# Attention and two MLPs on one Trainium2 core: the first block's first-half products in whole float32, weights and inputs split into rounded parts behind it

## The chip, the cores and the metric

The kernel runs on one core of one Trainium2 chip. The metric is the device time of one execution in microseconds (us): the median over runs of the same program. The core has a matrix engine (TensorE, in the profile PE, with its weight loads listed apart as PEld), VectorE (DVE), ScalarE (ACT), GpSimd (POOL) and SyncE (SP), which here only issues DMAs. Each engine takes its instructions strictly in the order in which the program has them; they meet by semaphores.

## What is computed

Four batches of eight heads: 512 local queries that see a window of 32 keys to both sides and 32 global keys, and 32 global queries that see everything. The result, 2176 tokens of 512 columns, goes through a first MLP with a squared ReLU and a second one with a product of two projections:

```python
x = attn_out.transpose(0, 2, 1, 3).reshape(B * S, H * D)   # 2176 x 512
h = np.maximum(x @ w_in, 0.0)          # w_in 512 x 2048
x = h * h @ w_out                      # w_out 2048 x 512
a, b = x @ w1, x @ w2                  # 512 x 1024 each
y = (a * b @ w3) @ w_out2              # 1024 x 1024, 1024 x 512
```

## The kernel before

**Arithmetic.** Nearly every product is made with operands that are split in two: a part rounded to the type float32r and the rest, subtracted in float32 and rounded too. `PASSES` lists three products of such parts (high by high, high by low, low by high); they are summed in PSUM. So one float32 product of a 128x128 weight tile with a block of columns is three matmuls. `split_w` (lines 447 to 453) splits a weight unit of 128x512: a cast on ACT (L448) and a subtraction on DVE (L449). `split_x` (552 to 556) splits an operand: a cast on ACT (L554), a subtraction on DVE (L137), and a store of both parts to `xs_d` on SP's queue (L556). The first four head pairs' scores and all products with probabilities and values are made in float32 itself.

**Weights.** They come as 64-bit words. A unit of 128x512 weights takes a load of 512 KB (`load_w`, tile `wraw`, two buffers), two ACT instructions (`conv_a`, L424 and L427), two DVE instructions (`conv_b`, L432 and L437; the second one frees the `wraw` buffer, and the load of the unit after next is issued) and an addition on POOL (`conv_c`, L506), whose result is a float32 weight in the tile `wt`; then `split_w` into a tile of the ring `u1` (16 buffers). Units 0 to 7 are the first half of `w_in`, 8 to 15 the first half of `w_out`.

**Stages.** The 2176 columns are cut into eight blocks of 256 and 288, two for each batch. Pass one takes the first half of the hidden units through all blocks: `h_unit(i, f, f)` makes unit f of block i (12 matmuls into a PSUM tile `h`, of which there are two), its ReLU (ACT L569), the square's rounded part (ACT L570), the whole square (DVE L572) and the square's low part (DVE L137). `x_unit_a(i, d)` adds up eight units into one of four output tiles (24 matmuls, PSUM tile `x`, two of them), `end_a` copies it into `st` (ACT L683) and, after the fourth, stores it to `part_d`; `split_a` splits a quarter of the next block's input. Pass two does the second half, and the second MLP follows. The columns of a batch exist once its attention is done, so `merge` interleaves the attention of the next batch, which `cycle(j)` lists pair of heads by pair, with the MLP of this one. For pairs 4 to 15 the keys and queries come in a tile `kqraw`, six loads for each pair, are split on DVE (`emit_k`: L202, L137 with 1120 columns), and POOL collects the global queries (`qgp`, L256) before PE makes the global scores `sg` and the local ones `sc`.

**What sets the order.** The code lists steps; a scheduler of the framework then puts the instructions of each engine into a fixed row by its own model, apart from a few that are held in program order. So an edit moves instructions far from where it stands. Block 0 is done while the attention of pairs 0 to 3 still runs and the weights still arrive; the tiles `wraw` and `wt` stand in a pool `cv`, which is closed behind it, and `kqraw` takes its place.

Of the kernel before, what the change touches and what calls it, by code (L numbers as in the profile page):

```python
# [9 lines left out]
F32 = mybir.dt.float32  # L10
F32R = mybir.dt.float32r
BF16 = mybir.dt.bfloat16
I32 = mybir.dt.int32
U32 = mybir.dt.uint32
AF = mybir.ActivationFunctionType
ALU = mybir.AluOpType
# [39 lines left out]
NB = 288  # L56
# [4 lines left out]
def block(i):  # L61
    i %= NBLK
    return S * (i // 2) + HALF * (i % 2), HALF if i % 2 == 0 else S - HALF
# [7 lines left out]
RUNS = (0, 16, PAIRED + 16)  # L71
# [26 lines left out]
AT_BUFS, H_BUFS, X_BUFS, P_BUFS, KQ_BUFS, ST_BUFS, HL_BUFS = 4, 2, 2, 5, 4, 6, 14  # L98
# [3 lines left out]
def attention_mlp(ctx: ExitStack, tc: tile.TileContext, kq0, kq, vw, wts, mask, ident, out_d):  # L102
    nc = tc.nc
# [3 lines left out]
    def pool(name, side="left", **kw):  # L107
        return tc.tile_pool(name=name, bufs=1, side=side, reuse_waits="tile", **kw)

    one = ctx.enter_context(pool("one"))  # L110
    sb = ctx.enter_context(pool("sb"))
# [3 lines left out]
    ps = ctx.enter_context(tc.tile_pool(name="ps", bufs=1, space=PSUM))  # L115
# [20 lines left out]
    def split_lo(eng, lo, raw, hi):  # L136
        eng.tensor_tensor(out=lo, in0=raw, in1=hi.bitcast(F32), op=ALU.subtract)  # L137
# [8 lines left out]
    def chain(o, terms):  # L146
        for k, (w, x) in enumerate(terms):
            mm(o, w, x, start=(k == 0), stop=(k == len(terms) - 1))  # L148
# [255 lines left out]
    raw_t, mid_t, w_t = {}, {}, {}  # L404
# [39 lines left out]
    def unit(tag, dtype=F32R):  # L444
        return pools[tag].tile([128, 2, 512], dtype, tag=tag, name=tag, bufs=16)

    def split_w(t, cols, raw, held=False):
        nc.scalar.copy(t[:, 0, cols], raw)  # L448
        s = nc.vector.tensor_tensor(  # L449
            out=t[:, 1, cols], in0=raw, in1=t[:, 0, cols].bitcast(F32), op=ALU.subtract  # L450
        )
        if held:
            tc.keep_in_program_order(s)
# [3 lines left out]
    def add_up(x, tag, eng):  # L457

        a11, a12, a21, a22 = (x[:, m, 256 * k : 256 * (k + 1)] for m in range(2) for k in range(2))
        s = unit(tag, F32)  # L460
        s1, s2, s3, s4 = (s[:, m, 256 * k : 256 * (k + 1)] for m in range(2) for k in range(2))
        add = eng.tensor_tensor
        add(out=s1, in0=a21, in1=a22, op=ALU.add)
        add(out=s2, in0=s1, in1=a11, op=ALU.subtract)
        add(out=s3, in0=a11, in1=a21, op=ALU.subtract)
        add(out=s4, in0=a12, in1=s2, op=ALU.subtract)
        return s

    def split_blocks(key, n, x, s, tag, held=False):

        t = []

        def third(raw):
            t.append(unit(tag))
            split_w(t[-1], slice(0, 512), raw, held)

        def last():
            if n % 2 == 0:
                half_t[tag] = unit(tag)
            (p, q, r), h, at = t, half_t[tag], 256 * (n % 2)  # L480
            split_w(h, slice(at, at + 256), x[:, 1, 256:], held)
            blocks_w[key] = {1: (p, 0), 2: (p, 256), 5: (q, 0), 6: (q, 256), 7: (r, 0), 3: (r, 256), 4: (h, at)}

        return [*(lambda raw=raw: third(raw) for raw in (x[:, 0], s[:, 0], s[:, 1])), last]

    def conv_c(n):
        _, b, m = mid_t.pop(n)
        if n >= PAIRED:
            k, u = divmod(n - PAIRED, 2)
            if u == 0:  # L490
                both_t[k] = unit("u1", F32)
                if "s" in both_t:
                    o, x, s = both_t.pop("s")
                    nc.sync.dma_start(out=both_d[o], in_=x)
                    nc.sync.dma_start(out=sums_d[o], in_=s)
            nc.gpsimd.tensor_tensor(out=both_t[k][:, u].bitcast(I32), in0=b, in1=m, op=ALU.add)
            if u == 1:
                x = both_t.pop(k)
                s = add_up(x, "u1", nc.vector)
                if k < 4:  # L500
                    both_t["s"] = k, x, s
                else:
                    for f in split_blocks(FIRST[k - 4], k, x, s, "u1"):
                        f()
            return
        nc.gpsimd.tensor_tensor(out=b, in0=b, in1=m, op=ALU.add)  # L506
        t = w_t[n] = unit(UNITS[n])
        split_w(t, slice(0, 512), b.bitcast(F32))

    def conv(n):  # L510

# [11 lines left out]
    xh, g_t = {}, {}  # L523
# [19 lines left out]
    def x_parts(i, k, n):  # L543

        t = xb_t[i, k] = fixed[4 * (i % 2) + k] if fixed else parts(NB)
        return t[:, :, :n]
# [5 lines left out]
    def split_x(i, k, src):  # L552
        t = xh[i, k] = x_parts(i, k, src.shape[-1])
        nc.scalar.copy(t[:, 0], src)  # L554
        split_lo(nc.vector, t[:, 1], src, t[:, 0])
        nc.sync.dma_start(out=of_split(i, k), in_=t.bitcast(F32))  # L556
# [5 lines left out]
    def h_unit(i, f, w):  # L562
        n = block(i)[1]
        h = ps.tile([128, 512], F32, tag="h", name="h", bufs=H_BUFS)[:, :n]
        w = w_t[w]
        chain(h, [(w[:, a, 128 * k : 128 * (k + 1)], xh[i, k][:, b]) for k in range(4) for a, b in PASSES])
        r = sb.tile([128, NB], F32, tag="tmp", name="r", bufs=4)[:, :n]
        g = g_t[f] = fixed[8 + f % 6][:, :, :n] if fixed else parts(n)
        nc.scalar.activation(r, h, AF.Relu)  # L569
        nc.scalar.activation(g[:, 0], r, AF.Square)  # L570
        if i < SHARED:
            nc.vector.scalar_tensor_tensor(  # L572
                out=r, in0=h, scalar=0.0, in1=r, op0=ALU.max, op1=ALU.mult
            )
        else:
            nc.scalar.activation(r, r, AF.Square)  # L576
        split_lo(nc.vector, g[:, 1], r, g[:, 0])

    st_t = {}

# [83 lines left out]
    def xcols(i):  # L664
        s, n = block(i)
        s -= S * (i // 2)
        return x_t[i // 2][:, :, s : s + n]

    steps = first_part()
    merge(steps, ([lambda n=n: conv(n) for n in range(8)], 0, len(steps) - 2))  # L670
    for k in range(4):
        split_x(0, k, xcols(0)[:, k])
    for i in range(4):
        load_pair(i, 1)
    for i in range(4):
        load_v(i)
    steps = [f for j in range(-1, 4) for f in cycle(j, ahead=j < 3)]
    main = [lambda f=f: h_unit(0, f, f) for f in range(8)]
    merge(steps, (main, 8, len(steps)), ([lambda n=n: conv(n) for n in range(8, 16)], 2, len(steps)))


    def end_a(i, d, o):
        (nc.scalar.copy if d < 2 or i < SHARED else nc.vector.tensor_copy)(staged(i, d), o)  # L683
        if d == 3:
            nc.sync.dma_start(out=of(part_d, i), in_=st_t[0])

    def split_a(i, d):
        if i < NBLK:
            split_x(i, d, xcols(i)[:, d])
        else:  # L690
            load_split(0, d)

    def x_unit_a(i, d):
        end_a(i, d, x_chain(i, d, range(8, 16)))
        split_a(i + 1, d)

    def load_x(i):

# [7 lines left out]
    for i in range(0, NBLK, 2):  # L706
        main = []
        for j in (i, i + 1):
            if j >= SHARED:
                if j == SHARED:  # L710
                    main.append(fix_places)
                main += rows(
                    j, 0, 8, lambda d, j=j: split_a(j + 1, d), lambda d, j=j: end_a(j, d, acc[d])
                )
                continue
            if j > 0:
                main += [lambda f=f, j=j: h_unit(j, f, f) for f in range(8)]
            main += [lambda d=d, j=j: x_unit_a(j, d) for d in range(4)]
        b = i // 2 + 1
        if b < B:  # L720
            if b == 1:
                cv_cm.__exit__(None, None, None)
                cv_cm = pool("sp")
                pools["cv"] = cv_cm.__enter__()
                load_kq(H // 2)
                for k in range(H, H + 4):
                    load_v(k)
            steps = [s for j in range(4 * b - 1, 4 * b + 4) for s in cycle(j, j < 4 * b + 3, j >= 4 * b)]
            fills = [(steps, 0, len(main) - 5)]
        else:  # L730
            for cm in (at_cm, rot_cm, cv_cm):
                cm.__exit__(None, None, None)
            pools["u2"] = ctx.enter_context(pool("u2", "right"))
            cv_cm = pool("cv2")
            pools["cv"] = cv_cm.__enter__()
            extra["w"] = sb.tile([128, 8 * NB], F32, tag="xb", name="wx", bufs=2)
            for k in range(16, 19):
                load_w(k)
            main.insert(18, lambda: load_x(0))
            fills = [([lambda n=n: conv(n) for n in range(16, 30)], 0, len(main))]  # L740
        merge(main, *fills)
# [159 lines left out]
    main = []  # L901
# [128 lines left out]
    main = []  # L1030
# [133 lines left out]
```

## Time and profile before

| | us |
|---|---|
| median of 3 runs | 866.93 (865.88 to 870.29) |
| the profiled execution | 866.06 |
| its span, first to last instruction | 864.2 |
| PE busy | 831.1 (96%), 6664 matmul records |
| DVE, ACT, POOL busy | 595.5 (69%), 490.6 (57%), 219.5 (25%) |
| mean granted TensorE clock | 0.988 of 2.4 GHz |

A busy PE in these tables means that a matmul was in flight; at half the granted clock it is as busy and does half the work. Matmul records overlap, since a matmul begins before the one ahead of it is out of the array, so what a matmul costs in a row of them is read from starts, not from durations. A float32 product shows as two records of one instruction.

### The profile page before, as it was taken

What the parts mean: (1) busy time and instruction counts of PE and PEld (TensorE: products, weight loads), DVE (VectorE), ACT (ScalarE), POOL (GpSimd) and SP (SyncE); (2) the same over time, 40 slices, a digit from 0 to 9 for tenths busy, and PEclk for the clock granted to TensorE, in tenths of its full rate; (3) what the DMA queues carried; (4) which work ended last, traced back from release to release, by engine and by line L of the source; (5) the groups of instructions that cost most, each with busy time, mean ns of one, the idle gap of its engine ahead of it and who ended that gap; (6) DMA issues with size and microseconds to landing.
All of it is one profiled execution on the core that took longest, in us unless ns stands there. A gap on an engine that the chain in (4) does not pass through costs nothing. (4 is left out here: it accounts for less than half of the span.)

```text
span 864.2 us, 17966 instructions
## 1 busy us (share of the span) xinstructions
PE 831.1 (96%) x6664; PEld 792.6 (92%) x6664; DVE 595.5 (69%) x1617; ACT 490.6 (57%) x1317; POOL 219.5 (25%) x264
## 2 busy tenths in 40 slices
PE   5789899999999999999999999999999999999998
PEld 3578899899999999999999999999999999999998
DVE  6998776777565667577646227795995757789772
ACT  5886666767565768777667346867321211255650
POOL 2342100100001022223233102330367554542000
PEclk9889999999999999999999999999999999999999
DMA  7753623343305058556756339755327643749941
GB/s 254 233 174 89 184 64 105 107 128 92 109 29 174 29 192 272 189 196 180 239 163 227 112 106 328 256 184 176 126 89 254 224 145 123 264 141 319 348 151 52
DMA packets 85303, 147.51 MB, mean 171 GB/s; under 512 B 6112, under 2 KB 58464, under 8 KB 85216
## 3 DMA queue, kind: packets, MB, share of 16 engines
q1 hardware_dynamic: 85216, 146.37, 50.8%
q8 instruction: 52, 0.85, 0.4%
q14 instruction: 35, 0.29, 0.1%
HBM read 100.07 MB, written 46.27 MB: 169 GB/s over the span
## 5 line engine op out<-in xcount | busy, mean ns | idle before, releaser
L148 PE MATMUL h<-hl,u 128*128 128x288 f32 (+1 forms) x1536 | 234.8, 296 | 3.8 <-DVE r L572 1.6
L148 PEld LDWEIGHTS h<-hl,u 128*128 128x128 f32 x1536 | 209.1, 192 | 11.0 <-DVE r L572 2.0
L786 PE MATMUL m<-hl,u 128*128 128x272 f32 x1296 | 172.6, 288 | 2.2 <-DVE r L808 1.1
L786 PEld LDWEIGHTS m<-hl,u 128*128 128x128 f32 x1296 | 165.4, 188 | 4.1 <-DVE r L808 1.7
L605 PE MATMUL acc<-hl,u 128*128 128x256 f32 (+1 forms) x960 | 139.3, 288 | 0.0
L605 PEld LDWEIGHTS acc<-hl,u 128*128 128x128 f32 x960 | 128.2, 188 | 1.3 <-DVE st L769 0.2
L506 POOL TENSOR_TENSOR wt<-wt 128x512 int32<-128x512 int32 x56 | 75.4, 1347 | 198.9 <-DVE wt L437 144.5
L137 DVE TENSOR_TENSOR hl<-r,hl 128x288 fp32r<-128x288 f32 (+1 forms) x128 | 73.4, 577 | 56.5 <-ACT r L576 55.2
L148 PE MATMUL x<-hl,u 128*128 128x288 f32 (+1 forms) x576 | 86.8, 295 | 1.0 <-ACT hl L570 0.9
L569 ACT ACTIVATE r<-h 128x288 f32<-128x288 f32 (+1 forms) x128 | 49.7, 391 | 59.5 <-PE h L148 58.9
L148 PEld LDWEIGHTS x<-hl,u 128*128 128x128 f32 x576 | 76.5, 189 | 3.5 <-ACT hl L570 1.4
L223 ACT ACTIVATE p<-p,st 128x224 f32<-128x224 f32 (+1 forms) x128 | 58.8, 462 | 24.8 <-DVE st L219 24.8
L786 PE MATMUL m<-u,u 128*128 128x272 f32 x528 | 71.1, 287 | 1.3 <-ACT u L1098 1.1
L786 PEld LDWEIGHTS m<-u,u 128*128 128x128 f32 x528 | 67.6, 188 | 2.1 <-ACT u L1098 1.3
L449 DVE TENSOR_TENSOR u<-wt,u 128x512 fp32r<-128x512 f32 x56 | 43.5, 779 | 34.5 <-ACT u L448 33.8
L256 POOL CAST qgp<-kq_hl 64x32 fp32r<-64x32 f32 x48 | 19.5, 406 | 174.2 <-PE sg L148 152.7
L570 ACT ACTIVATE hl<-r 128x288 fp32r<-128x288 f32 (+1 forms) x128 | 54.8, 430 | 7.4 <-issue 2.8
L803 ACT COPY r<-m 128x272 f32<-128x272 f32 x40 | 15.4, 385 | 76.0 <-PE m L786 76.0
L949 POOL TENSOR_TENSOR rs<-rs 128x272 f32<-128x272 f32 x64 | 57.4, 907 | 2.9
L219 DVE CUSTOM_DVE_ANT_0 p<-sc,mask_sb 128x224 f32<-128x224 f32 (+1 forms) x128 | 40.6, 368 | 16.3 <-PE sc L142 16.0
L948 POOL TENSOR_TENSOR rs<-rs 128x272 f32<-128x272 f32 x32 | 28.4, 889 | 90.8 <-DVE rs L816 90.8
L305 PE MATMUL tp<-ident_sb,p 128*128 128x128 f32 x256 | 39.4, 292 | 10.0 <-DVE p L231 8.2
(107 smaller groups left out, 1292.6 us busy)
## 6 DMA issues: line engine op xcount, KB each, us to landing
wraw<-in_wts SPq DMA_DIRECT2D x53, 512.0 KB, 4.2
q_d<-rs SPq DMA_DIRECT2D x16, 952.0 KB, 5.2
rl<-q_d SPq DMA_DIRECT2D x12, 1088.0 KB, 6.0
wx<-in_wts SPq DMA_DIRECT2D x19, 512.0 KB, 3.5
v_f<-in_vw SPq DMA_DIRECT2D x24, 256.0 KB, 2.9
xs_d<-hl SPq DMA_DIRECT2D x16, 288.0 KB, 4.2
hl<-xs_d SPq DMA_DIRECT2D x16, 288.0 KB, 4.4
x2l<-x_d SPq DMA_DIRECT2D x4, 1088.0 KB, 6.4
```

The source lines that it names most:

```text
L137: eng.tensor_tensor(out=lo, in0=raw, in1=hi.bitcast(F32), op=ALU.subtract)
L148: mm(o, w, x, start=(k == 0), stop=(k == len(terms) - 1))
L219: nc.vector.tensor_tensor_reduce(out=p[:, c], in0=sc[:, n, w], in1=mask_sb[:, t, m], scale=-SCALE, scalar=3.0e38, op0=ALU.add, op1=ALU.min ...
L223: nc.scalar.activation(p[:, c], p[:, c], AF.Exp, bias=least[:, n : n + 1], scale=-1.0, accum_out=sums[:, n, 0:1],)
L305: nc.tensor.transpose(tp[:, k, :], p[:, at : at + 128], ident_sb)
L449: s = nc.vector.tensor_tensor(out=t[:, 1, cols], in0=raw, in1=t[:, 0, cols].bitcast(F32), op=ALU.subtract)
L506: nc.gpsimd.tensor_tensor(out=b, in0=b, in1=m, op=ALU.add)
L569: nc.scalar.activation(r, h, AF.Relu)
L570: nc.scalar.activation(g[:, 0], r, AF.Square)
L605: mm(acc[d], w[:, a, 128 * d : 128 * (d + 1)], g_t[f][:, b], start=(f + k == 0), stop=(f + k == 9),)
L786: mm(o, w, x, start=(i in (1, 6, 5, 4) and k == 0), stop=(k == len(terms) - 1), skip_group_check=(i in (2, 7, 3)),)
L949: sub = lambda o, a, c: nc.gpsimd.tensor_tensor(out=o, in0=a, in1=c, op=ALU.subtract)
```

## The change

Units 0 to 15 are no longer split as they arrive: POOL's addition writes the float32 weight into a `u1` tile, two units to a tile (units 14 and 15 stay in `wt`). Block 0 has functions of its own: `h_whole` multiplies these weights by the unsplit columns (4 float32 matmuls for the 12), and makes the square with a ReLU on ACT and one DVE instruction, without parts; `x_whole` adds up eight of them (8 float32 matmuls for the 24). The input of block 0 isn't split ahead of it. Behind each `x_whole(d)` two units of `w_in` are split (`split_late`), and `behind(f)`, called after each unit of block 1, splits a unit of `w_out` and, at every second, a quarter of block 0's columns, whose parts pass two needs.

```diff
+        if n < RUNS[1]:
+            if n < 14 and n % 2 == 0:
+                whole_t[n // 2] = unit("u1", F32)
+            whole = whole_t[n // 2][:, n % 2].bitcast(I32) if n < 14 else b
+            nc.gpsimd.tensor_tensor(out=whole, in0=b, in1=m, op=ALU.add)
+            w_whole[n] = whole.bitcast(F32)
+            return
         nc.gpsimd.tensor_tensor(out=b, in0=b, in1=m, op=ALU.add)
         t = w_t[n] = unit(UNITS[n])
         split_w(t, slice(0, 512), b.bitcast(F32))
+
+    def split_late(n):
+        w_t[n] = unit("u1")
+        split_w(w_t[n], slice(0, 512), w_whole.pop(n))
+        if n % 2 == 1:
+            whole_t.pop(n // 2, None)
...
+    def h_whole(f):
+        x = xcols(0)
+        n = x.shape[-1]
+        h = ps.tile([128, 512], F32, tag="h", name="h", bufs=H_BUFS)[:, :n]
+        chain(h, [(w_whole[f][:, 128 * k : 128 * (k + 1)], x[:, k]) for k in range(4)])
+        r = sb.tile([128, NB], F32, tag="tmp", name="r", bufs=4)[:, :n]
+        g_t[f] = sb.tile([128, 2, NB], F32, tag="hl", name="hl", bufs=HL_BUFS)[:, 0, :n]
+        nc.scalar.activation(r, h, AF.Relu)
+        nc.vector.scalar_tensor_tensor(
+            out=g_t[f], in0=h, scalar=0.0, in1=r, op0=ALU.max, op1=ALU.mult
+        )
+
+    def x_whole(d):
+        o = ps.tile([128, 512], F32, tag="x", name="x", bufs=X_BUFS)[:, : block(0)[1]]
+        chain(o, [(w_whole[8 + f][:, 128 * d : 128 * (d + 1)], g_t[f]) for f in range(8)])
+        end_a(0, d, o)
+        split_a(1, d)
+        split_late(2 * d)
+        split_late(2 * d + 1)
...
-    for k in range(4):
-        split_x(0, k, xcols(0)[:, k])
...
-    main = [lambda f=f: h_unit(0, f, f) for f in range(8)]
+    main = [lambda f=f: h_whole(f) for f in range(8)]
...
+    def behind(f):
+        split_late(8 + f)
+        if f % 2 == 1:
+            split_x(0, f // 2, xcols(0)[:, f // 2])
...
-            if j > 0:
-                main += [lambda f=f, j=j: h_unit(j, f, f) for f in range(8)]
+            if j == 0:
+                main += [lambda d=d: x_whole(d) for d in range(4)]
+                continue
+            main += [lambda f=f, j=j: (h_unit(j, f, f), behind(f) if j == 1 else None) for f in range(8)]
             main += [lambda d=d, j=j: x_unit_a(j, d) for d in range(4)]
```

Lines behind the edit stand up to 48 lines lower: L449 and L137 keep their numbers, L569 of block 0 becomes L603, L572 becomes L604, the stores of a split L572, the copy of `st` L724, its store L726.

The scheduler's rows differ from before only up to some 420 instructions into DVE's row and 865 into PE's; behind that every engine has the same row. Three places follow.

DVE's row where units 5 to 8 of the weights arrive, at about 29 to 38 us; `wt` and `wraw` are the conversion, `u` the split unit, `hl` the split input of block 0, `stg` the global softmax. Before:

```order
L449 TENSOR_TENSOR u_313<-wt,u_313 128x512
L432 TENSOR_SCALAR wt<-wt 128x512
L437 SCALAR_TENSOR_TENSOR wt<-wraw,wt 128x512
L137 TENSOR_TENSOR hl<-xb,hl 128x256
L449 TENSOR_TENSOR u_341<-wt,u_341 128x512
L432 TENSOR_SCALAR wt<-wt 128x512
L437 SCALAR_TENSOR_TENSOR wt<-wraw,wt 128x512
L137 TENSOR_TENSOR hl<-xb,hl 128x256
L449 TENSOR_TENSOR u_368<-wt,u_368 128x512
L432 TENSOR_SCALAR wt<-wt 128x512
L273 TENSOR_REDUCE stg_91<-sg 64x1
L437 SCALAR_TENSOR_TENSOR wt<-wraw,wt 128x512
```

The same place in the changed kernel:

```order
L432 TENSOR_SCALAR wt<-wt 128x512
L437 SCALAR_TENSOR_TENSOR wt<-wraw,wt 128x512
L432 TENSOR_SCALAR wt<-wt 128x512
L437 SCALAR_TENSOR_TENSOR wt<-wraw,wt 128x512
L432 TENSOR_SCALAR wt<-wt 128x512
L437 SCALAR_TENSOR_TENSOR wt<-wraw,wt 128x512
L273 TENSOR_REDUCE stg_91<-sg 64x1
L432 TENSOR_SCALAR wt<-wt 128x512
L273 TENSOR_REDUCE stg_91<-sg 64x1
L437 SCALAR_TENSOR_TENSOR wt<-wraw,wt 128x512
```

The subtractions L449 and L137 between the conversions are gone from here; thirteen of the sixteen L449 of these units stand further on in the row, yet ahead of the split of block 1's second quarter of columns, and nine of them ahead of the conversion of unit 14.

SP's row of DMA issues where pair 4's loads `kqraw` stand (`xs_d` takes split inputs, `v_f` are values). Before:

```order
L418 DMA wraw<-in_wts 128x1024 x5
L196 DMA v_f_618<-in_vw 128x384
L196 DMA v_f_620<-in_vw 128x384
L418 DMA wraw<-in_wts 128x1024
L186 DMA kqraw<-in_kq 64x256
L187 DMA kqraw<-in_kq 64x288
L188 DMA kqraw<-in_kq 64x576
```

In the changed kernel:

```order
L418 DMA wraw<-in_wts 128x1024
L572 DMA xs_d<-hl 128x2x288
L196 DMA v_f_699<-in_vw 128x384
L196 DMA v_f_701<-in_vw 128x384
L572 DMA xs_d<-hl 128x2x288
L196 DMA v_f_906<-in_vw 128x512
L196 DMA v_f_908<-in_vw 128x512
L572 DMA xs_d<-hl 128x2x288
L726 DMA part_d<-st 512x1x256
L186 DMA kqraw<-in_kq 64x256
```

The loads moved from right behind the last weight load to behind the store of block 0's output `part_d`; on ACT the copy that this store waits for stands directly behind the casts of units 13 to 15.

PE's row where pair 4's scores begin (`sg` global, `sc` local); `u_202` and `u_229` before, `u_929` and `u_932` after, are the first two weight units in block 1's products. Before:

```order
L148 MATMUL sg<-kq_hl,qgp 128x288 x3
L148 MATMUL sg<-kq_hl,qgp 128x256 x3
L142 MATMUL sc<-kq_hl 128x192 x6
L142 MATMUL sc<-kq_hl 128x224 x6
L148 MATMUL h<-hl,u_202 128x288
L148 MATMUL h<-hl,u_229 128x288
L148 MATMUL h<-hl,u_202 128x288 x2
L148 MATMUL h<-hl,u_229 128x288 x2
```

In the changed kernel:

```order
L148 MATMUL h<-hl,u_929 128x288
L148 MATMUL h<-hl,u_932 128x288
L148 MATMUL h<-hl,u_929 128x288 x2
L148 MATMUL h<-hl,u_932 128x288 x2
L148 MATMUL sg<-kq_hl,qgp 128x288
L148 MATMUL sg<-kq_hl,qgp 128x256
L142 MATMUL sc<-kq_hl 128x192 x2
L148 MATMUL x<-hl,u_1304 128x288 x2
```

The last quarter of block 1's first two units now stands ahead of pair 4's scores, and 24 matmuls of its next two units follow behind them, where before pair 4's second scores and pair 5's first ones came.

## Rows read from the trace of the kernel before

**Rows 1.** The span in stretches: busy us by engine, clock, DMA share, GB/s.

```profile
0.00:33.00 33.00, 17.64 (x112) 13.51 (x112) 24.50 (x83) 24.19 (x64) 9.96 (x32) 0.92 0.67 227
33.00:80.00 47.00, 40.17 (x290) 34.14 (x287) 43.62 (x126) 35.98 (x100) 18.01 (x16) 0.87 0.47 158
80.00:112.00 32.00, 29.82 (x264) 27.13 (x263) 23.53 (x94) 19.11 (x67) 5.25 (x12) 0.95 0.58 173
...
160.00:300.00 140.00, 139.46 (x1293) 130.66 (x1291) 96.94 (x406) 92.58 (x307) 11.41 (x24) 1.00 0.28 91
```

**Rows 2.** Timeline near 16 us: start, length, what, [idle before].

```profile
15.64 1.28 DVE L449 TENSOR_TENSOR u<-wt,u 128x512 fp32r<-128x512 f32 x2
...
17.30 0.46 ACT L223 ACTIVATE p<-p,st 128x192 f32<-128x192 f32 x1 [1.29 <-DVE st L219]
```

**Rows 3.** PE's timeline, two stops between 33 and 80 us.

```profile
41.60 0.51 PE L148 MATMUL h<-hl,u 128*128 128x256 f32 x2 [1.25 <-ACT hl L554]
...
46.02 0.77 PE L292 MATMUL tg<-ident_sb,pg 64*128 64x64 f32 x5 [2.78 <-ACT p L223]
```

**Rows 4.** Groups by line, DVE and ACT: total us, mean ns of one.

```profile
L449 DVE TENSOR_TENSOR u<-wt,u 128x512 fp32r<-128x512 f32 x56 | 43.5, 779 | 34.5 <-ACT u L448 33.8
...
L137 DVE TENSOR_TENSOR hl<-r,hl 128x256 fp32r<-128x256 f32 x64 | 35.4, 556 | 24.6 <-ACT r L576 24.2
...
L448 ACT CAST u<-wt 128x512 fp32r<-128x512 f32 x56 | 34.5, 616 | 14.8 <-POOL wt L506 14.7
...
L570 ACT ACTIVATE hl<-r 128x256 fp32r<-128x256 f32 x64 | 26.5, 416 | 3.6 <-issue 1.7 <-ACT wt L427 0.8
```

**Rows 5.** The same view, from 33 to 80 us alone.

```profile
L449 DVE TENSOR_TENSOR u<-wt,u 128x512 fp32r<-128x512 f32 x12 | 12.4, 1033 | 0.0
```

**Rows 6.** ACT's waits up to 112 us: total, times, longest.

```profile
ACT wt L424 <- DMA wraw<-in_wts: 6.0, 5, 2.3
```

**Rows 7.** DMA issues: count, KB each, median us to landing.

```profile
wraw<-in_wts SPq DMA_DIRECT2D x53, 512.0 KB, 4.2
```

**Rows 8.** PE's timeline near 62 and 78 us.

```profile
62.41 1.58 PE L148 MATMUL h<-hl,u 128*128 128x256 f32 x12
63.82 0.63 PE L148 MATMUL x<-hl,u 128*128 128x256 f32 x4
...
77.96 1.18 PE L148 MATMUL sg<-kq_f,qgf 128*128 128x288 f32 x4
78.80 1.06 PE L148 MATMUL x<-hl,u 128*128 128x256 f32 x6
79.69 0.43 PE L148 MATMUL h<-hl,u 128*128 128x288 f32 x2
```

**Rows 9.** PE's timeline, end of block 0 to pair 5.

```profile
91.52 1.04 PE L305 MATMUL tp<-ident_sb,p 128*128 128x128 f32 x8
...
94.77 1.02 PE L148 MATMUL sg<-kq_hl,qgp 128*128 128x288 f32 x6
...
96.93 1.06 PE L148 MATMUL h<-hl,u 128*128 128x288 f32 x6
...
103.09 4.97 PE L148 MATMUL h<-hl,u 128*128 128x288 f32 x24 [1.61 <-DVE r L572]
```

**Rows 10.** Timeline of pair 4's operands, 79 to 87 us.

```profile
78.91 0.48 SPq L186 DMA_DIRECT2D kqraw<-in_kq  x1
...
80.07 0.60 SPq L188 DMA_DIRECT2D kqraw<-in_kq  x1
...
83.06 0.74 DVE L202 CAST kq_hl<-kqraw 128x1120 fp32r<-128x1120 f32 x1 [0.76 <-DMA kqraw<-in_kq]
...
83.87 2.35 POOL L256 CAST qgp<-kq_hl 64x32 fp32r<-64x32 f32 x4 [12.18 <-DVE stg L283]
```

**Rows 11.** Single microseconds behind two stops.

```profile
48.00:49.00 1.00, 1.00 (x5) 0.82 (x3) 1.00 (x2) 1.00 (x4) 0.85 (x2) 0.50 0.66 238
...
104.00:105.00 1.00, 1.00 (x6) 1.00 (x6) 1.00 (x5) 0.00 (x0) 0.21 (x1) 0.50 0.00 0
```

More of the change, by code (lines that the diff above doesn't have):

```diff
@@ L508, in conv_c @@
         split_w(t, slice(0, 512), b.bitcast(F32))
+    whole_t, w_whole = {}, {}
+    def split_late(n):
[3 more added lines that the diff above has]
+            whole_t.pop(n // 2, None)
     def conv(n):
@@ L577, in h_unit @@
         split_lo(nc.vector, g[:, 1], r, g[:, 0])
+    def h_whole(f):
[11 more added lines that the diff above has]
+        o = ps.tile([128, 512], F32, tag="x", name="x", bufs=X_BUFS)[:, : block(0)[1]]
+        chain(
+            o,
+            [
+                (w_whole[8 + f][:, 128 * d : 128 * (d + 1)], g_t[f])
+                for f in range(8)
+            ],
+        )
+        end_a(0, d, o)
+        split_a(1, d)
+        split_late(2 * d)
+        split_late(2 * d + 1)
     st_t = {}
```

## The prediction

> **What bounds the kernel now.** I read the span in stretches first [rows 1]: behind 112 us PE is busy throughout at full clock (139.5 of 140 us in the stretch shown, and so to the end in the slices of the page), and the engines' rows are unchanged behind about 140 us. So the change is worth what it moves in the first 112 us, and that is passed on whole to the end. Up to 33 us PE is busy for 17.6 of 33 us, from 33 to 80 for 40.2 of 47 at a mean clock of 0.87. In both stretches DVE is the fullest: 24.5 of 33 and 43.6 of 47 us. PE's own stops show the same: at 41.60 it waits for a split of block 0's input, at 46.02 for a softmax on ACT that stood behind conversions [rows 3]. Behind 80 us PE is the bound but for one stop of 1.61 us at 103.09 [rows 9]. The profiled execution took 866.06 us, 0.87 below the median of the runs; the sum is made on it and the 0.87 added at the end.
>
> **Part 1, to the first product of block 0 at 33 us.** At 15.64 two splits of weights hold DVE for 1.28 us, the score reductions behind them are late, and ACT then idles 1.29 us for these [rows 2]. In the changed kernel no split stands there, nor the two later ones of this stretch. Of that chain I take 1.2 us, and half as much again for the later ones: 2 us, between 1 and 3.
>
> **Part 2, from 33 to 80 us.** By the time block 1's first products start (79.69, [rows 8]) DVE has before done 16 L449, eight low parts of squares and four of the input. After, 13 of the L449 are still ahead of that point: the scheduler brings most of the splits forward again. DVE loses 3 x 0.78 + 12 x 0.56 = 9.0 us, ACT 3 x 0.62 + 12 x 0.42 = 6.9 us (the input's parts priced like the squares' of the same 256 columns) [rows 4]. More may go: in this stretch an L449 takes 1033 ns for a mean of 779, beside the additions on POOL [rows 5], and nothing says whether another instruction will meet these instead.
> Two things eat into it. First, units 5 to 8 of the weights now follow each other on DVE with next to nothing between. A buffer of `wraw` takes 4.2 us to land [rows 7] and about 2 us until DVE has read it, and there are two: a unit every 3.1 us. ACT already waits 6.0 us for these loads [rows 6]. Some 2 us of DVE's relief becomes such waiting.
> Second, the products themselves. Twelve split matmuls of 256 columns take from 62.41 to 63.82, 0.1175 us each, so the three that stand for one product 0.35. Two float32 products `sg<-kq_f` (288 and 256 columns, four records) and six split ones run from 77.96 to 79.69; less 6 x 0.1175 that leaves 1.02 us for 544 columns, 0.48 for 256 [rows 8]. From start to start alone it would be 0.84 us, 0.40 for 256, but the six behind it then take 0.15 each, so I take 0.48 and keep 0.40 as the lower end. A product is 0.13 us dearer: 64 x 0.13 = 8.3 us of PE (3.0 at the lower end). Of the 64, 48 stand in this stretch (8 units of h, two of four output tiles): 6.2 us more work for PE. It has 6.8 us of stops (47 - 40.2) and what the low clock costs (at most 47 x 0.13 = 6.1, part of it within the stops) to take that from, so it is hidden only if the stops really go.
> The Trainium skill ("FP8 and Floating Point Precision", TensorE Precision Notes) says that true FP32 takes four passes through the array. At 4 x 0.1175 that is an estimate of 0.47 for a product and 7.5 us for 64; the 1.02 us of the trace agree, and by the page the sum would be better by 0.2 us.
> With DVE relieved by 7 to 9 us and PE loaded with 6 more, both come out nearly full. I take 4 us of gain at block 1's start, part 1 included; 0 if PE becomes the bound, 8 if DVE's relief counts whole.
>
> **Part 3, the end of block 0.** The last 16 products (two output tiles) lie where PE is full: 16 x 0.13 = 2.0 us against. The end of block 0's `x`, 91.52 before [rows 9], comes at 91.5 - 4 + 2 = 89.5.
>
> **Part 4, the loads of pair 4.** This is the place where I expect the gain to go. Before, pair 4's first loads go out at 70.30 and the last at 80.07 (0.58 us apart), DVE's cast runs at 83.06, and `sg` at 94.77 waits for nothing [rows 9, 10]. In the changed kernel SP has these six loads behind the store to `part_d`, and that waits for the copy of block 0's last tile. SP can't pass it; behind it queue also pair 5's loads. From the end of `x`: a copy 0.4 (as ACT's of 256 columns, [rows 4]), the store's issue 0.6, five issues of 0.58, from the last issue's start to the cast 3.0 (83.06 - 80.07), the cast 0.7, two of the four POOL copies 1.2 [rows 10]: 8.8 us. `sg` can start at 98.3. Before it started at 94.77, with one more piece of block 1 behind it (1.0 us from 96.93, [rows 9]) that now stands ahead: 95.8 is the like of it. So 2.5 us are lost here, and PE, whose row has only 4.2 us of work between, stands still for 4.6 us.
> The Trainium skill ("DMA: Bandwidth & Descriptors", the fixed cost) puts about 2.0 us on a transfer whatever its size. By that estimate `sg` would start 1.0 us sooner; the trace's 3.0 decides.
>
> **Part 5, the clock, and the old stop.** Behind the stop at 41 to 46 us the granted clock is 0.50 (1.2 GHz), and again behind the one at 103.09 [rows 11]; there 24 products of 288 columns take 4.97 us [rows 9] for some 3.3 at full clock (24 x 0.1175 x 288/256 = 3.2), so that such a stop costs 1.7 us more. The new stop costs that, up to 3.2 if the half clock lasts twice as long. In return the old stop and its half clock (1.61 + 1.7 = 3.3) should not come again: PE now has the 24 products of the next two units there, which don't need the crowded DVE at once. If they are held up after all, nothing is returned. Net +1.65, between -3.2 and +3.3.
>
> **Sum.** -2.5 + 1.65 = 0.9 us slower: 867.0 on the profiled execution, with 0.87 **867.8**. That is no change: about 0.5% (4.3 us) is what a measurement here can tell from none. Block 0's low parts and the four late splits of the input (0.56 us each on DVE) fall behind 100 us, where DVE has slack (23.5 of 32 us busy from 80 to 112, [rows 1]); without that cover they cost their 2.2 us.
>
> **Rivals.**
> *Slower: PE becomes the bound of the early stretch.* For it: 6.2 us more of float32 products in a stretch that has 40 of 47 us busy, in order, with whole groups waiting for weights 14 and 15, which arrive no sooner than the loads let them. Against: its stops are DVE's. Then block 1 starts no earlier, `x` ends at 93.5, `sg` starts at 102.3, 6.5 lost; the stop is long and the half clock costs 3.2, with 3.3 returned: 6.4 slower, **873.3**. It counts as slower once `x` ends behind 93 us. Chance 0.27.
> *Faster: DVE's relief counts whole.* The L449 no longer meet POOL's additions, 8 us are gained, `x` ends at 85.5, `sg` starts at 94.3: 1.5 won and the old stop's 3.3 too, with hardly a half clock: 4.8, **862.1**. Against it: the splits that come back early, and the loads' pace. Chance 0.16.
> *The change doesn't put the splits behind.* Nine of sixteen stand ahead of unit 14's conversion, so that DVE is as full from 45 to 70 us as before, and only part 1's 2 us remain: `x` at 91.5, `sg` at 100.3, 4.5 lost and 1.65 returned, **869.8**, still no change by the bound. Chance 0.15.
> The forecast has 0.42.
>
> **How the numbers follow.** Faster by over 0.5% is the second rival, at its edge, 0.15; slower the first, 0.27; the rest, 0.58, within. The range goes from the second rival's 862 to 873, just short of the first one's time; some 0.2 lie outside, mostly above. The forecast's own is 865 to 870.
>
> **What would show it.** In the changed trace: L449 and ACT's waits gone from 15 us; DVE waiting for ACT's L424 and ACT for `wraw` near 30 to 40 us; float32 products 0.48 us apart; block 0's last `x` near 89.5; `kqraw` issued right behind `part_d`; PE idle for 4 to 5 us before `sg<-kq_hl`, DVE's cast waiting for that load, and some 3 us at 0.50 behind. I am wrong if `sg<-kq_hl` waits for nothing, if the old stop at 103 us stays, or if the rest of the span, from 140 us on, is not as long as before.

## The result, and the profile after

The changed kernel takes **872.62 us** (median, 870.45 to 875.77), the kernel before 866.66 (863.34 to 870.29): a ratio of 1.0068, 95% interval 1.0047 to 1.0090. It is 5.9 us or 0.7% slower; the median lies beyond the 0.5% that were called no change, the lower end of the interval just under it. The forecast was 867.8, 4.8 us less than measured; its range, 862 to 873, holds the time at its upper edge. The time is that of the slower rival (873.3), the trace is not.

The same stretches as [rows 1], in the changed kernel (columns: stretch, its length, busy us of PE, PEld, DVE, ACT and POOL with their instructions, PE's granted clock, DMA share, GB/s):

```profile
0.00:33.00 33.00, 20.26 (x136) 15.09 (x136) 20.92 (x79) 21.63 (x58) 11.20 (x33) 0.90 0.71 243
33.00:80.00 47.00, 40.86 (x243) 32.28 (x240) 40.61 (x119) 35.60 (x98) 13.91 (x15) 0.93 0.41 134
80.00:112.00 32.00, 25.87 (x184) 21.75 (x183) 17.74 (x65) 13.48 (x44) 3.07 (x8) 0.84 0.46 138
...
160.00:300.00 140.00, 139.23 (x1306) 129.70 (x1305) 95.79 (x404) 90.95 (x301) 12.21 (x28) 1.00 0.31 99
```

DVE lost 3.6 us up to 33 us and 3.0 from 33 to 80. Up to block 1's first product it was busy for 67.8 us before and for 60.7 after, so 7.1 us were lost where 9.0 were forecast (ACT: 60.2 and 55.1, so 5.0 for 6.9). PE gained 2.6 and 0.7 us of busy time there and lost 4.0 of 32 us from 80 to 112, at a clock of 0.84 instead of 0.95. From 160 us on it is full again. So the loss is made before that and handed on.

Two marks on PE's timeline cut this more finely: block 1's first product (the first `h` of 288 columns) and pair 7's last `sg`. For each stretch I added up, microsecond by microsecond, what PE stood idle and what the low clock took (busy time times one minus the granted clock); the rest is work at full clock. Two of the experiments below stand beside it.

| | to block 1's first product: time = idle + low clock + work | from there to pair 7's last `sg` |
|---|---|---|
| before | 79.69 = 22.19 + 7.24 + 50.26 | 200.47 = 3.76 + 1.66 + 195.05 |
| changed | 77.21 = 18.88 + 6.10 + 52.23 | 208.99 = 9.29 + 3.71 + 195.98 |
| E1, loads early | 77.17 = 20.04 + 3.09 + 54.04 | 201.72 = 3.80 + 1.70 + 196.22 |
| E5, splits held too | 71.97 = 15.91 + 1.71 + 54.35 | 200.40 = 3.76 + 1.71 + 194.93 |

The change wins 2.5 us up to block 1 and loses 8.5 behind it, 5.5 of these as idle time and 2.0 by the clock. (The low clock of the first stretch differs between profiles of the same row: 2.73 us of the changed kernel's 6.10 stand ahead of 27 us, where E1 has none. A profile is one execution. E5's took 857.45 us, the shortest of its runs and 3.6 under their median, so its row shows the gain too large.)

**Where the 8.5 us go.** The timeline of the changed kernel at the end of block 0 (start, length, engine, what, how often, [idle before and what ended it]):

```profile
88.48 1.03 PE L148 MATMUL x<-hl,wt 128*128 128x256 f32 x4
...
89.94 0.60 SPq L726 DMA_DIRECT2D part_d<-st  x1
90.60 1.80 SPq L186 DMA_DIRECT2D kqraw<-in_kq  x1
92.44 0.60 SPq L187 DMA_DIRECT2D kqraw<-in_kq  x1
...
94.63 1.29 PE L148 MATMUL h<-hl,u 128*128 128x288 f32 x6 [1.19 <-ACT hl L570]
...
95.01 0.59 SPq L188 DMA_DIRECT2D kqraw<-in_kq  x1
...
98.18 0.74 DVE L202 CAST kq_hl<-kqraw 128x1120 fp32r<-128x1120 f32 x1 [3.12 <-DMA kqraw<-in_kq]
98.99 2.43 POOL L256 CAST qgp<-kq_hl 64x32 fp32r<-64x32 f32 x4 [28.00 <-DVE kq_hl L202]
...
100.67 0.82 PE L148 MATMUL sg<-kq_hl,qgp 128*128 128x288 f32 x2 [4.76 <-DVE r L588]
```

The last `x` of block 0 ends at 89.16 (the next group's start). The six loads of pair 4 go out behind `part_d`, the cast waits for the last of them, and `sg`, which before stood at 94.77 and waited for nothing [rows 9], starts at 100.67 behind a stop of 4.76 us. The releaser named there is only the last of several; the chain through the cast is what was late. Behind the stop PE works for 7.3 us, up to 108, at half the clock (0.50, 1.2 GHz); the two ends in single microseconds:

```profile
101.00:102.00 1.00, 1.00 (x5) 0.58 (x4) 1.00 (x4) 0.00 (x0) 0.42 (x1) 0.50 0.63 177
...
107.00:108.00 1.00, 1.00 (x6) 1.00 (x6) 1.00 (x8) 0.00 (x0) 0.41 (x2) 0.50 0.00 0
108.00:109.00 1.00, 1.00 (x8) 0.87 (x7) 1.00 (x7) 0.78 (x3) 0.00 (x0) 0.95 0.26 68
```

**Why the early gain is small.** The splits were to come behind block 0. The group of L449 from 33 to 80 us (us in all, mean ns of one):

```profile
L449 DVE TENSOR_TENSOR u<-u,u 128x512 fp32r<-128x512 f32 x13 | 10.0, 802 | 0.1
```

Before there were 12 for 12.4 us [rows 5]. And they stand in the way, as the timeline shows:

```profile
58.68 2.98 DVE L449 TENSOR_TENSOR u<-u,u 128x512 fp32r<-128x512 f32 x3
61.58 0.77 DVE L273 TENSOR_REDUCE stg<-sg 64x1 f32<-64x288 f32 x2
...
62.67 0.41 DVE L604 SCALAR_TENSOR_TENSOR hl<-h,r 128x256 f32<-128x256 f32 x1
...
63.13 3.24 PE L148 MATMUL h<-xb,u 128*128 128x256 f32 x8 [2.72 <-DVE hl L604]
```

Three splits hold DVE for 2.98 us, a square (L604) that frees the PSUM tile of the next unit waits behind them and behind the softmax reductions (L273) that had queued there too, and PE stops for 2.72 us. What DVE gained in front of this went in part into waiting: up to 112 us it waited 7.0 us for ACT's half of the conversions (L424), before 3.0.

**What a float32 product costs.** On PE's timeline four of 256 columns (eight records) run from 47.46 to 49.18, six from 78.79 to 81.47:

```profile
47.46 1.89 PE L148 MATMUL h<-xb,u 128*128 128x256 f32 x8
49.18 1.03 PE L148 MATMUL x<-hl,u 128*128 128x256 f32 x4
...
78.79 2.75 PE L148 MATMUL x<-hl,u 128*128 128x256 f32 x12
81.47 0.64 PE L142 MATMUL sc<-kq_f 64*128 64x224 f32 x2
```

That is 0.43 and 0.45 us for one, against 0.35 for three split matmuls [rows 8]: 0.08 to 0.10 us more, or 5 to 6 us for 64.

### The profile page after: what moved, and what is told of

Its sections match the earlier page's. It is cut to its first block, busy times and chain, and to the rows that moved or that the text cites. A ratio compares the mean times of both kernels' runs of the same rounds, so it can differ in the third digit from the quotient of the medians.

```text
span 871.0 us, 17838 instructions
## 1 busy us (share of the span) xinstructions
PE 834.9 (96%) x6600; PEld 791.2 (91%) x6600; DVE 589.8 (68%) x1609; ACT 488.3 (56%) x1309; POOL 216.6 (25%) x264
## 5 line engine op out<-in xcount | busy, mean ns | idle before, releaser
L148 PE MATMUL h<-hl,u 128*128 128x288 f32 (+1 forms) x1440 | 217.8, 293 | 3.1 <-DVE hl L137 1.3
L148 PEld LDWEIGHTS h<-hl,u 128*128 128x128 f32 x1440 | 194.4, 190 | 8.7 <-DVE hl L137 1.9
L137 DVE TENSOR_TENSOR hl<-r,hl 128x288 fp32r<-128x288 f32 (+1 forms) x120 | 69.5, 583 | 57.0 <-ACT r L592 56.0
L513 POOL TENSOR_TENSOR wt<-wt 128x512 int32<-128x512 int32 x40 | 52.3, 1306 | 158.6 <-DVE wt L437 125.8
L585 ACT ACTIVATE r<-h 128x288 f32<-128x288 f32 (+1 forms) x120 | 47.0, 395 | 63.4 <-PE h L148 62.8
L223 ACT ACTIVATE p<-p,st 128x192 f32<-128x192 f32 (+1 forms) x128 | 59.0, 465 | 36.2 <-DVE st L219 36.2
L256 POOL CAST qgp<-kq_hl 64x32 fp32r<-64x32 f32 x48 | 19.1, 398 | 182.0 <-PE sg L148 132.6
L586 ACT ACTIVATE hl<-r 128x288 fp32r<-128x288 f32 (+1 forms) x120 | 51.6, 432 | 7.3 <-issue 2.8
L219 DVE CUSTOM_DVE_ANT_0 p<-sc,mask_sb 128x192 f32<-128x192 f32 (+1 forms) x128 | 40.6, 368 | 21.9 <-PE sc L142 21.8
L449 DVE TENSOR_TENSOR u<-wt,u 128x512 fp32r<-128x512 f32 x42 | 29.1, 692 | 35.3 <-ACT u L448 34.6
L802 PE MATMUL wacc<-u,u 128*128 128x512 f32 x192 | 48.0, 391 | 0.0
```

The costliest lines, as they stand in the source:

```text
L219: nc.vector.tensor_tensor_reduce(out=p[:, c], in0=sc[:, n, w], in1=mask_sb[:, t, m], scale=-SCALE, scalar=3.0e38, op0=ALU.add, op1=ALU.min ...
L223: nc.scalar.activation(p[:, c], p[:, c], AF.Exp, bias=least[:, n : n + 1], scale=-1.0, accum_out=sums[:, n, 0:1],)
L449: s = nc.vector.tensor_tensor(out=t[:, 1, cols], in0=raw, in1=t[:, 0, cols].bitcast(F32), op=ALU.subtract)
L802: mm(o, w3[:, a, 128 * q : 128 * (q + 1)], w_t[32 + 4 * half + q][:, b], start=(half + q + k == 0), stop=(half + q + k == 6),)
```

## The experiments

**Theory:** the loss is pair 4's loads behind `part_d`. **Rival F:** PE's float32 work. **Rival S:** late splits that run early. A ratio's interval is about 0.2% to each side, so a difference of two of them is good to some 2.4 us. Differences between variants are taken from their ratios, times 866 us, because the kernel before was timed anew beside each group of them (medians of 865.47 to 866.66). The marks come from one profiled execution of each kernel. Behind pair 7's last `sg` the rows are the same in all, and yet PE stood idle there for 6.7 us (E5) to 11.0 us (E4), so a few us of a kernel's time can lie in the execution and not in the marks.

| kernel | block 1's first product | block 0's `x` done | pair 4's first `sg` | pair 7's last `sg` | median | ratio to before (95%) |
|---|---|---|---|---|---|---|
| before | 79.69 | 91.52 | 94.77 | 280.16 | 866.66 | |
| changed | 77.21 | 89.16 | 100.67 | 286.20 | 872.62 | 1.0068 (1.0047 to 1.0090) |
| E1 loads early | 77.17 | 89.44 | 93.41 | 278.89 | 865.23 | 0.9990 (0.9971 to 1.0009) |
| E2 before, loads late | 78.08 | 90.76 | 101.48 | 281.27 | 870.08 | 1.0048 (1.0028 to 1.0068) |
| E3 E1, h alone | 77.06 | 93.62 | 95.98 | 283.08 | 870.62 | 1.0050 (1.0031 to 1.0069) |
| E4 E1, x alone | 76.92 | 89.05 | 92.95 | 277.88 | 866.84 | 1.0006 (0.9990 to 1.0023) |
| E5 E1, splits held | 71.97 | 85.12 | 87.67 | 272.37 | 861.03 | 0.9947 (0.9928 to 0.9965) |
| E6 E1, 16 products more in h | 79.31 | 91.40 | 95.36 | 281.29 | 870.50 | 1.0050 (1.0030 to 1.0070) |
| E7 E1, 16 more in x | 76.36 | 93.00 | 96.09 | 280.67 | 869.44 | 1.0048 (1.0031 to 1.0065) |
| E8 changed, splits held | 74.84 | 87.87 | 121.11 | 295.32 | 879.87 | 1.0156 (1.0126 to 1.0186) |
| E9 E4, splits held | 78.16 | 89.11 | 93.02 | 282.35 | 865.89 | 0.9997 (0.9977 to 1.0017) |
| E10 E3, splits held | 76.92 | 90.17 | 93.18 | 277.99 | 866.51 | 1.0007 (0.9992 to 1.0021) |
| E11 E5, DVE's held alone | 74.49 | 88.73 | 91.29 | 277.39 | 863.84 | 0.9971 (0.9949 to 0.9992) |
| E12 E5, 16 more in h | 81.78 | 91.46 | 95.98 | 281.35 | 868.85 | 1.0031 (1.0010 to 1.0053) |

### E1: the loads early again

In the changed kernel unit 15's float32 weights stay in the conversion pool `cv` until the last of the late splits. As I read its rows, the scheduler doesn't begin the next pool ahead of that split, though nothing on the chip waits for it: in E8 below the loads go out from 109.69 us on and the last split runs at 113.03. With these two units elsewhere the loads stand early in SP's row, as before.

```diff
-            whole = whole_t[n // 2][:, n % 2].bitcast(I32) if n < 14 else b
+            if n < 14:
+                whole = whole_t[n // 2][:, n % 2].bitcast(I32)
+            else:
+                whole = sb.tile([128, 2, NB], F32, tag="hl", name="wh", bufs=HL_BUFS)
+                whole = whole.rearrange("p a n -> p (a n)")[:, :512].bitcast(I32)
```

> The changed kernel with one edit: the whole weights of units 14 and 15 stand in a tile of the ring of splits of x and squares instead of in the conversion pool, so that the pool ends with unit 15's conversion and the six loads of pair 4's keys and queries stand on SP ahead of the x splits' stores and of part_d, as they do in the kernel before. Theory (the loss is pair 4's operands behind part_d): `sg` of pair 4 no longer stands last behind x of block 0; its stop of 4.76 us and the half clock behind it go, at most a stop of about 1.6 us comes back; between the last x of block 0 and the store that stood at 187.25 us, 13.0 us of idle and low clock fall to 5 to 8. Time 864.5 to 868, so 5 to 8 us under the changed kernel. Rival F (float32 products are the loss, PE bounds the early stretch): 0 to 2 us come back, 870.5 to 872.5. Rival S (late splits on DVE and ACT are what PE waits for): the stop only changes its releaser from the transfer to DVE or ACT, 870 to 872.

Measured: 865.23, by the ratios 6.8 us under the changed kernel, as the theory said. Its timeline:

```profile
68.26 0.59 SPq L186 DMA_DIRECT2D kqraw<-in_kq  x1
...
71.44 0.60 SPq L188 DMA_DIRECT2D kqraw<-in_kq  x1
...
76.09 0.72 DVE L202 CAST kq_hl<-kqraw 128x1120 fp32r<-128x1120 f32 x1
...
93.41 1.02 PE L148 MATMUL sg<-kq_hl,qgp 128*128 128x288 f32 x6
...
101.73 3.70 PE L148 MATMUL h<-hl,u 128*128 128x288 f32 x15 [1.61 <-DVE r L591]
```

`sg` waits for nothing, and the stop of 1.61 us that before stood at 103.09 [rows 9] is back, with its 1.7 us of low clock. What is left of the change can't be told from the kernel before.

### E2: the kernel before with the loads late

```diff
         end_a(i, d, x_chain(i, d, range(8, 16)))
+        if i == 0 and d == 3:
+            nc.vector.tensor_tensor(
+                out=held_sb, in0=st_t[0][:, d, :2], in1=held_t[15].bitcast(F32)[:, :2], op=ALU.add
+            )
```

> The kernel before with one addition of 128x2 elements on DVE, which reads unit 15's converted weights together with the last x staging tile of block 0, so that the conversion pool is held until then and pair 4's six loads stand behind part_d on SP, as in the changed kernel; its products and splits stay as they were. Theory (the loads' place alone makes the loss): part_d is issued about 97 us, the loads behind it, and `sg` comes some 9 to 11.5 us behind the last x, at 102 to 108 us instead of 94.8; PE stops for 4 to 8 us and runs a few us at half clock: 5 to 9 us slower, 871.5 to 876. Rival F or S: the loads' place matters little, because PE has other products there: within 2 us of the kernel before, 865 to 869.

Measured: 870.08, 4.2 us slower by the ratio. That is between the two expectations, 1.4 us under the theory's and 1.1 above the rivals'. Its timeline repeats the changed kernel's:

```profile
91.36 0.61 SPq L687 DMA_DIRECT2D part_d<-st  x1
92.02 0.62 SPq L187 DMA_DIRECT2D kqraw<-in_kq  x1
...
94.37 1.28 PE L149 MATMUL h<-hl,u 128*128 128x288 f32 x6 [1.19 <-ACT hl L556]
...
98.60 0.74 DVE L203 CAST kq_hl<-kqraw 128x1120 fp32r<-128x1120 f32 x1 [1.64 <-DMA kqraw<-in_kq]
...
101.48 0.41 PE L149 MATMUL sg<-kq_hl,qgp 128*128 128x288 f32 x2
```

The place of the loads alone costs time in a kernel that has nothing else of the change; less than 6.8 us, since here some 20 more products of block 1 stand ahead of `sg`: PE idled 2.9 us where the changed kernel idles 6.1, and in this profile no half clock follows up to pair 7's last `sg`. So the theory holds from both sides, though at a smaller price here than it named: the loads' place is the loss.

### E3, E4: one half alone in float32

> Only the first half's products (h) of block 0 in float32, with pair 4's loads early; the squares are split and x of block 0 is made from split weights (units 8 to 15 split at their conversion, as before). Theory: the early gain of the first product (33.3 to about 27 us) stays, the x products cost 12 us less work on PE's own clock against 14 in float32 (32 products x 0.44 against 96 x 0.116 us), and DVE and ACT get back the 8 early splits of units 8 to 15 and 8 of squares, which hold x: first product of block 1 between 77 and 80 us; time 863 to 867. If what the change gains early is DVE's and ACT's relief in the x half, the time is that of the kernel before or worse: 866 to 869.

> Only the second half's products (x) of block 0 in float32, with pair 4's loads early; weights 0 to 7 and x are split early as before, the squares are not split and units 8 to 15 are split late. Theory: the first product of block 0 stays at about 33 us, as before; the 8 splits of units 8 to 15 and of squares leave DVE and ACT between 45 and 80 us, so block 1's first product comes 1 to 3 us earlier than before, 77 to 79; x costs about 2 us more on PE: time 865 to 868. If float32 products are the main loss, this one is slower than the variant with h alone by 2 us or more.

I expected E3 to be the better one, and it is the worse, 870.62 us and above both of its ranges: 5.2 us over E1 by the ratios, `x` done 4.2 us later. The squares and units 8 to 15 have to be split there ahead of `x`, on top of the late splits that run early. E4 is within its range and no different from before. Dropping half of the float32 products brought nothing.

### E5: the late splits held

The 2 tells `split_w` to keep the split's two instructions, ACT's cast and DVE's subtraction, where the program lists them.

```diff
-        split_w(w_t[n], slice(0, 512), w_whole.pop(n))
+        split_w(w_t[n], slice(0, 512), w_whole.pop(n), 2)
```

> The variant with pair 4's loads early, and its 16 late splits kept in the order in which the program writes them on ScalarE and VectorE, so that none of them runs ahead of block 0's x products as 9 of VectorE's did there. Rival S (late splits that run early hold DVE and ACT, and so PE): the stop of 3.7 us before an `h` product that is released by DVE's softmax and the one of 1.6 behind it shrink, block 1's first product comes 1 to 3 us earlier than 77.2, 862 to 864.5. Theory (the splits fill time that DVE and ACT have, PE waits for the weights' conversions): no gain; the splits now stand beside block 1's products and pair 4's softmax, 865 to 869.

My theory expected no gain. Measured: 861.03, 3.7 us under E1 and 0.5% under the kernel before: this version beats both. The group of L449 from 33 to 80 us, and the stretch:

```profile
L449 DVE TENSOR_TENSOR u<-u,u 128x512 fp32r<-128x512 f32 x4 | 2.7, 687 | 0.0
```

```profile
33.00:80.00 47.00, 44.11 (x270) 35.11 (x272) 39.00 (x124) 32.96 (x99) 15.26 (x19) 0.96 0.53 168
```

E1 has 13 splits in this stretch and E5 four; PE is busy for 44.1 us instead of 40.5, and block 1's first product comes at 71.97 instead of 77.17. E1's stretch, and a stop of PE in it that in E5 is gone:

```profile
33.00:80.00 47.00, 40.47 (x241) 32.22 (x238) 40.60 (x118) 35.36 (x98) 16.47 (x19) 0.93 0.46 148
...
61.73 3.78 PE L148 MATMUL h<-xb,u 128*128 128x256 f32 x8 [3.72 <-DVE st L227]
```

Rival S is right about the early stretch, beside the theory.

### E6, E7, E12: 7 us of PE work more

The additional products are written over by the unit's own.

> The variant with pair 4's loads early, with 16 float32 products of 256 columns more in block 0's h half (two more at the head of each of the 8 units, written over by the unit's own): 16 x 0.44 = 7.0 us of PE work more, between 26 and 70 us, where PE stood idle for 8.5 us. If PE's work bounds the early stretch (rival F): +5 to +7 us, 870 to 872. If DVE, ACT and the weights' loads bound it: 0 to +2.5 us, 865 to 867.7.

> The same with 16 float32 products more in block 0's x half (four more at the head of each of its 4 chains): 7.0 us of PE work more, in 70 to 89 us, where PE hardly waits. Expected if the x half is PE's own: +5 to +7 us, 870 to 872; if it waits for the squares and conversions there: +2 to +4.

> The variant with pair 4's loads early and both engines' splits held, with 16 float32 products more (7.0 us of PE work) in block 0's h half. Without holding these had cost 5.3 us. With the splits held PE is busy for 44.1 of the 47 us from 33 to 80, so if PE is now the bound there: +6 to +8, 867 to 869. If the weights' loads and conversions still hold block 0: +2 to +4, 863 to 865.

By the ratios they cost 5.2 and 5.0 us on E1 and 7.3 on E5, for 7.0 us of work. The traces show less for the first two: at pair 7's last `sg` E6 is 2.4 us behind E1 and E7 1.8, and the rest of the difference lies in no mark; E12 is 9.0 behind E5, whose profile is a short one. So rival F has its part. With the splits held all of such work is on the path; without, by the marks a quarter to a third, by the times up to three quarters, and how much is left open. What the surcharge of 5 to 6 us for the float32 products themselves costs was not run apart; by these shares it is an estimate of 1 to 4 us.

### E8: held splits without the early loads

> The changed kernel with the held splits alone: pair 4's loads still stand behind part_d. Holding the splits took 4.2 us off where the loads were early. If the two causes add up: 868 to 869, with block 1's first product near 72 us and `sg` of pair 4 some 11 us behind block 0's last x, 95 to 97 us. If the gain of the held splits is lost in the wait for pair 4's loads (the chain starts at the last x, and the work that PE has ahead of `sg` is no more than before): 870 to 872.

Worse than either expectation: 879.87, 7.6 us over the changed kernel. Holding unit 15's split holds the pool in the scheduler's order, and SP's row has more ahead of the loads (timeline; the split itself is the line of DVE):

```profile
88.66 0.60 SPq L728 DMA_DIRECT2D part_d<-st  x1
...
92.13 17.51 SPq L574 DMA_DIRECT2D xs_d<-hl  x4
109.69 0.99 SPq L186 DMA_DIRECT2D kqraw<-in_kq  x1
...
113.03 0.69 DVE L449 TENSOR_TENSOR u<-wt,u 128x512 fp32r<-128x512 f32 x1
...
121.11 0.41 PE L148 MATMUL sg<-kq_hl,qgp 128*128 128x288 f32 x2
```

The first load leaves 19.1 us later than in the changed kernel, `sg` starts 20.4 us later; PE fills much of it with products of block 1 and has none left behind: 35.9 of 48 us busy from 112 to 160.

```profile
112.00:160.00 48.00, 35.93 (x303) 29.88 (x303) 33.22 (x141) 25.29 (x90) 7.90 (x20) 0.89 0.44 125
```

The two causes do not add up: the same hold is worth 3.7 us with the loads early and costs 7.6 with them late.

### E9, E10, E11: which part of the hold

> Only the x half of block 0 in float32, pair 4's loads early, and the 8 late splits held in program order. 7 us more of float32 work in the h half had cost 5.3, so half of the float32 products less (32 x 0.06 us = about 2 us of PE work) is worth some 1.5; against it the first product comes at 31 us, not 26. If the held splits are what counts: 861 to 863, like the held variant with both halves. If the 8 early splits of units 0 to 7 and of x (some 8 us of DVE) bound the stretch: 865 to 867, as without holding.

> Only the h half in float32, pair 4's loads early, its 8 late splits held. It was 870.6 unheld, 5.4 over the variant with both halves in float32. If early-run splits of units 0 to 7 were that loss: 863 to 866. If the splits of units 8 to 15 and of the squares, which x needs in either order, are the loss: 868 to 871, and PE still waits for them at 60 to 92 us.

> The variant with pair 4's loads early and held splits, but only VectorE's subtractions held; ScalarE's casts of the weights (0.62 us each) may run ahead again, and 9 of them do, beside the conversions near 55 us. If VectorE's early subtractions (13 in 52 to 74 us) were what stopped PE: about 861, as with both held. If ScalarE's casts, which stand ahead of conversions and softmax, were it: about 865, as with none held, and PE waits for ACT at 50 to 65 us.

Holding makes E10 3.7 us faster than E3, as E5 is than E1, though E10's 866.51 lies just above the range that was named for this. E9 gains nothing on E4, where five of the eight late splits had run ahead (at 55 to 62 us). So what counts seem to be units 0 to 7, whose splits ran ahead in E1 and E3; one comparison on each side shows it, good to 2.4 us. Neither half alone comes near E5; each leaves 8 splits that are needed early. E11 lies between: 1.6 us under E1, 2.1 over E5, each within what the intervals allow as none; PE's stops there are on DVE's softmax (1.68 us at 61.24) while ACT casts 11 units between 33 and 80 us. That both engines' splits matter is likely, not shown.

## Where the forecast held and where it missed, point by point

The time lies inside the range, but "no change" was wrong. In the terms of the sum, `sg` came 2.4 us later than forecast (part 4), the half clock cost 2.0 us more (part 5), and 2.1 us of new stops were in no term (part 5); that is 6.5 us, close to the 5.9 by which the growth of the span (6.8) exceeds the forecast one (0.9). That the time is still inside is in part luck: the edge at 873 was drawn from the slower rival, whose path the trace doesn't show.

- **The frame** held in the main: what is late at pair 7's last `sg` (6.0 us) is nearly what the span is longer (864.2 to 871.0, 6.8). But not all of it arises in the first 112 us, as was assumed: the new stops of part 5 lie behind.
- **Part 1** (2 us): block 0's first product came at 27.04 instead of 33.30, but behind it ACT waits for the weights' loads (4.35 us in four waits from 25 to 37 us) and PE stops for ACT's copies that stand behind these; as a gain for the end it can't be told apart.
- **Part 2** (4 us at block 1's start): 2.5. The 9.0 us leave the 13 early splits out rightly; the step that failed is to count DVE's relief as a sum, wherever in its row it falls, although these 13 were known to stand ahead. They hold squares and softmax, and PE with them. Nor did PE's stops "show the same" as DVE's busy time: both that were quoted [rows 3] were ended by ACT. E5's first product of block 1 comes 7.7 us earlier than before, near the 8 that stood for "DVE's relief counts whole" (6.3 less idle time and 5.5 less by the clock, against 4.1 more work); its median gives 4.6. The price of a float32 product, taken at 0.48 us, is 0.43 to 0.45, so 5 to 6 us for 64, not 8.3. The four passes that the Trainium skill gives ("FP8 and Floating Point Precision", TensorE Precision Notes) made an estimate of 0.47; the measured ones are a little under it.
- **Part 3**: `x` done at 89.16, forecast 89.5. Right by luck: the gain ahead of it was 1.5 us smaller, and the way from block 1's first product to there took 11.95 us after 11.83, where 2.0 were to be added.
- **Part 4**: the right place, under-sized. From `x` to `sg` 11.5 us instead of 8.8: the first load's issue took 1.80 us, not 0.58; the copy and store took 0.4 more, POOL's share 0.5 more, small gaps the rest. `sg` at 100.67, not 98.3; PE idle for 6.0 us (1.19 and 4.76), not 4.6. The place costs 6.8 us (E1); the prediction's own price for it is some 3 us, the 4.6 of idle time less the net 1.65 that part 5 was to give back.
- **Part 5**: the old stop did go, as forecast. But the half clock behind the new one costs 3.71 us, above the 3.2 of the upper end, and new stops come at 150 to 161 us (0.39, 0.68, 1.27 and 0.77, so 3.1 in all; before 0.45 and 0.60).
- **The rivals.** The slower one named the time and the wrong mark: it wanted `x` behind 93 us, and it ended at 89.2. Its reason has a part of open size (E6, E7). "The splits come back" (869.8) was true as a mechanism and had `sg` near its place (100.3), but for another reason: its `x` at 91.5 was 2.3 us too late, and part 4's chain too short.

## What to carry over

Work that is moved later in a program leaves an engine only if it really lands later: count it in the built row, and hold it there if the scheduler brings it forward. A tile that lives a little longer can keep a whole pool from its successor, and with it loads that have nothing to do with the change. Causes that meet in one queue do not add: against the changed kernel the early loads alone won 6.8 us, the held splits alone lost 7.6, and both together won 10.5 and were the fastest version of all.

## What the runs showed of the hardware

A float32 matmul of 256 columns took 0.43 to 0.45 us, 1.25 times three split ones. One issue of a 64x256 load on SP took 1.80 us where its neighbours took 0.6; in E2, at the same place in the row, it took 0.62. What made it long stays open.
